# Batch 0's z and w2 transposed by DMA instead of by TensorE, in a Fourier filter with a maxout MoE

## The chip, the cores and the metric

The kernel runs on one core of a Trainium2 chip. A core has TensorE (PE; the profile shows its weight loads apart as PEld), VectorE (DVE), ScalarE (ACT), GpSimd (POOL) and SyncE (SP), which here only issues DMAs. The metric is device time in microseconds (us) of one execution; a median is taken over several. Profiled executions are told by their span, from the first to the last instruction.

## What is computed

```
X = np.fft.rfft(x, axis=1)                        # x: 8 batches, 3072 positions, 256 channels
Y = X * (filt_r + 1j * filt_i)[None, :, :]
x2 = np.fft.irfft(Y, n=3072, axis=1).reshape(24576, 256)
g = np.maximum(x2 @ w1, x2 @ w2)                  # hidden width 1024
out = g @ w_out                                   # 24576 x 256, float32
```

## The kernel before

The Fourier transform of 3072 points is split as 96 x 32 and done by matmuls with tables of sines, in bf16: a stage of 96 points, a stage of 32 points, the product with the filter, and the two stages back. For batches 1 to 7 the axes change places by DMAs through DRAM (`ad` and `zd`). Batch 0 has nothing to hide such a round trip behind, so it changes axes on TensorE: `s1t` and `t1` on the way in, `s3t` and `t2` on the way back.

`s3t(v, ...)` (L560, v = 0 to 5) is the third stage of batch 0. It leaves z with channels in the partitions; ACT and, for half of v = 4 and 5, DVE copy it from PSUM to the tile `zT` (128 partitions; two channel halves, 32 positions m, 96 values k). `t2(c, engines)` (L582, c = 0 to 7) turns the eight 128 x 96 squares of four positions on PE and copies them to `zr[0]` (96 partitions). `s4(tt)` (L454) does the last stage for tile tt of batch 0: eight matmuls of `zr[0]` with the table `G1`, copied by ACT and DVE to `y`. A batch has eight tiles of 384 positions, and tile tt needs just what `t2(tt)` wrote.

The MoE of a tile follows. Since max(a, b) = b + max(a - b, 0), `moe_h` (L476) computes relu(y (w1 - w2)) in eight blocks j, and `moe_o` (L501) adds this times w_out and y times M, where M = w2 w_out. `prep_m` (L308) makes M with 16 matmuls from `w2T`, the transposed w2: its first eight use the first half of the channels, its last eight the second. `prep_t(jp)` (L300) makes `w2T`: eight PE transposes and an ACT copy for each of two halves of the hidden axis. The input of these, `w2b`, is w2 cast to bf16 by POOL (`cast_w2`, L290), behind POOL's other set-up work. The result of `moe_o` is copied from PSUM to `ot`, and `out_block` (L491) writes it to DRAM: by POOL's queue, for the last two tiles by SP's.

The order of all this is written out by hand. Every engine runs its instructions in the order in which the program gives them. Set-up and batch 0's transform come first; then a loop runs over tiles and their eight blocks, and a step is 8 times the tile's number in its batch plus the block. At each step `moe_h` of this tile and `moe_o` of the tile before are issued, and what two tables, `mid` and `todo`, hold for the step. In batch 0 they hold, among others: `t2` of 1 at step 1, of 2 at step 7, of 3 at step 8, of 4 to 7 at steps 22, 32, 40 and 48; `prep_t` at steps 7 and 8; `prep_m` at step 9; `f1` (L323), the first stage of batch 1, whose results SP writes to `ad`, up to step 13; then `f1_read` (L340), which reads them back; the `visit`s of batch 1's middle stages from step 25; loads of batch 2's x into `XF` by SP (`load_xf`, L91) and their folding by POOL (`fold`, L101). `s4` of the next tile is issued at a tile's block 4. `s4g` is the last stage for batches 1 to 7; that of batch 1 reads what SP wrote to `zd` and read back.

Pools: the buffers of set-up (`init`, and `pq0` for the products) are given back by `setup.close()` (L686), and the pools opened behind it use their place. `zT` has one of two buffers of `bpool` before.

Of the kernel before, what the change touches and what calls it, by code (L numbers as in the profile page):

```python
# [8 lines left out]
FP32 = mybir.dt.float32  # L9
BF16 = mybir.dt.bfloat16  # L10
# [17 lines left out]
def kernel(  # L28
# [16 lines left out]

    const = ctx.enter_context(tc.tile_pool(name="const", bufs=1))
    C1 = const.tile([NP, 96], BF16)
    G1 = const.tile([96, NP], BF16)
    U = const.tile([128, NU, 64], BF16)
    VP = const.tile([128, NW, 2, 64], BF16)  # L50
    VQ = const.tile([128, NW, 2, 64], BF16)
# [18 lines left out]
    pso = ctx.enter_context(tc.tile_pool(name="pso", bufs=2, space=bass.MemoryType.PSUM))  # L70
    zrpool = ctx.enter_context(tc.tile_pool(name="zrpool", bufs=2))
    setup = ExitStack()
    init = setup.enter_context(tc.tile_pool(name="init", bufs=1))
    pq0 = setup.enter_context(tc.tile_pool(name="pq0", bufs=6))
    ctx.enter_context(tc.manual_schedule())

    xb = {}
# [76 lines left out]
    jb = init.tile([128, 16], FP32)  # L154
    cid = init.tile([128, 128], FP32)

    hv = init.tile([128, 2, 1], FP32)
    load_x(0, 0, 1)
    G.iota(pid, pattern=[[1, 1]], base=0, channel_multiplier=1, allow_small_or_imprecise_dtypes=True)
# [32 lines left out]

    def table_ct():
        G.memset(CT, 0.0)
# [54 lines left out]
        S.activation(U[:, NW * h:NW * h + NW], uv[:, NW * h:NW * h + NW], AF.Sin, bias=zero, scale=TWO_PI)  # L249

    def table_g():
        pg = ps.tile([96, NP], FP32, tag="ps", name="pg")
        TE.matmul(pg, C1, I128[0:NP, 0:NP], start=True, stop=True)
        S.activation(G1, pg, AF.Copy)

    def table_v(h, q):
# [40 lines left out]
        js = slice(256 * q, 256 * q + 256)  # L297
        engine.tensor_tensor(Wd[:, :, js], w1f[:, :, js], w2f[:, :, js], OP.subtract)

    def prep_t(jp):  # L300
        pt = ps.tile([128, 4, D], BF16, tag="ps", name="pt")
        for ji in range(4):
            for dc in range(2):
                j = 4 * jp + ji
                TE.transpose(pt[:, ji, 128 * dc:128 * dc + 128], w2b[:, dc, 128 * j:128 * j + 128], I128)
        S.activation(w2T[:, 4 * jp:4 * jp + 4], pt, AF.Copy)

    def prep_m():  # L308
        pm_ = ps.tile([128, 2, D], FP32, tag="ps", name="pm_")
# [144 lines left out]
    def s4(tt):  # L454
        b, i = divmod(tt, 8)
        y_ = ypool.tile([128, 2, 384], BF16, tag="yt", name="y_")
        for dc in range(2):
            py = ps.tile([128, 4, NP], FP32, tag="ps", name="py")
            for m in range(4):
                TE.matmul(py[:, m], zr[b][:, 4 * i + m, 128 * dc:128 * dc + 128], G1, start=True, stop=True)  # L460
# [30 lines left out]
    def out_block(tt, c):  # L491
        b, i = divmod(tt, 8)
        dst = out[b * N:(b + 1) * N].rearrange("(c p i m) d -> c i p (m d)", c=3, p=32, i=8)[c, i]
        E = G if tt < 8 * B - 2 else nc.sync
        E.dma_start(out=dst, in_=ot[tt // 2][:, 3 * (tt % 2) + c])  # L495


    FIRST = ([(c, e) for c in (0, 2) for e in range(8)] + [(c, e) for c in (0, 2) for e in (8, 9)]
             + [(1, e) for e in range(10)])

    def moe_o(tt, k0, k1):  # L501
        y_, g_ = yt[tt], gt[tt]
        for k in range(k0, k1):
            c, e = divmod(k, 10) if tt else FIRST[k]
            n = e if tt else (e + 2) % 10
            q = 3 * tt + c
            blk = slice(128 * c, 128 * c + 128)
            if e == 0 and (q % 2 == 0 or q == 24 * B - 1):
# [6 lines left out]
            if e == 9 and q >= 24 * B - 2:  # L515
                e = q % 6
                if q % 2 == 0:
                    S.activation(ot[tt // 2][:, e], p_, AF.Copy, scale=SCALE)
                else:
                    S.activation(ot[tt // 2][:, e, 0:112], p_[:, 0:112], AF.Copy, scale=SCALE)  # L520
                    V.tensor_scalar(ot[tt // 2][:, e, 112:D], p_[:, 112:D], SCALE, None, OP.mult)
# [37 lines left out]

    def s3t(v, pq):  # L560
        pool, tag = (ps, "ps") if v % 2 else (pso, "po")
        pz = [pool.tile([128, 2, 2, 2, 2, NM], FP32, tag=tag, name="pt%d" % g) for g in range(2)]
        for _ in range(2 if v == 1 else 1):
            TE.matmul(pz[0].rearrange("p i s r c m -> p (i s r c m)"), W1[:, 0:128], W1, start=True, stop=True)
        for i in range(2):
            for s in range(2):
                for dc in range(2):
                    for q, tab in enumerate((VP, VQ)):
                        for g in range(2):
                            TE.matmul(pz[g][:, i, s, :, dc], pq[s][64 * g:64 * g + 64, q, i, 128 * dc:128 * dc + 128],  # L570
                                      tab[64 * g:64 * g + 64, 2 * v + i, s].rearrange("p (r m) -> p r m", r=2),
                                      start=(q == 0), stop=(q == 1))
        zv = zT.rearrange("p c m (w g) q -> p w g (c m) q", g=2)
        for g in range(2):
            o_ = zv[:, 2 * v:2 * v + 2, g]
            i_ = pz[g].rearrange("p i s r c m -> p i (c m) (s r)")
            if v >= 4 and g == 1:
                V.tensor_copy(o_, i_)
            else:
                S.activation(o_, i_, AF.Copy)  # L580

    def t2(c, engines):  # L582
        if c == 0:
            zr[0] = zrpool.tile([96, NM, D], BF16, tag="zr", name="zr")
        n = 4 // len(engines)
        for k, engine in enumerate(engines):
            pr = ps.tile([96, n, D], BF16, tag="ps", name="pr")
            m0 = 4 * c + n * k
            for m in range(n):
                for dc in range(2):  # L590
                    TE.transpose(pr[:, m, 128 * dc:128 * dc + 128], zT[:, dc, m0 + m].rearrange("p u q -> p (u q)"),  # L591
                                 I128)
            if engine is V:
                V.tensor_copy(zr[0][:, m0:m0 + n], pr)
            else:
                S.activation(zr[0][:, m0:m0 + n], pr, AF.Copy)

    def spin(n):
        for _ in range(n):
# [96 lines left out]
    f1(1, 1, V)  # L696
    spin(1)
    s4(0)
# [46 lines left out]
    for b in range(1, B):  # L745
# [59 lines left out]
```

## Time and profile before

| what | value |
|---|---|
| time, median of 3 runs (lowest, highest) | 499.26 us (497.63, 505.28) |
| time of the profiled execution | 500.08 us |
| its span | 498.3 us |
| PE busy in the span | 482.5 us, 97% |
| DVE, ACT, POOL busy | 336.0, 320.0, 257.9 us |
| batch 0's t2: PE matmuls | 64, 0.219 us each, from 36.7 to 89.3 us |
| its DVE copies | 8, 0.42 to 0.69 us |
| prep_t: PE matmuls | 16, 0.219 us each, from 42.7 to 45.2 us |
| its ACT copies | 2, 1.024 us each |
| prep_m: PE matmuls | 16, 0.272 us each, from 46.4 us |

How to read it: busy time is what the profile attributes to instructions; matmuls overlap, so eight transposes in a row take 0.61 us, not eight times 0.219. Rows of the timeline give the start, the length to the end of the last instruction of a merged row, engine, line, operation, written and read tile, shape and count; what stands in brackets at the end is the idle time before, and what ended it. The rows of the table by stage give the stretch, its length, then busy time and count for PE, PEld, DVE, ACT and POOL, the clock that PE was granted, the mean busy share of the 16 DMA engines, and what they moved in GB/s.

### The profile page before, as it was taken

To read this page: it belongs to the slowest core of one execution; us is meant where nothing else is said; L and a number is where in the kernel's file an instruction comes from. 1 tells how busy PE (TensorE), PEld (TensorE's weight loads), DVE (VectorE), ACT (ScalarE), POOL (GpSimd) and SP (SyncE) were. 2 spreads that over 40 slices of the span, in tenths; PEclk is the share of its full clock that TensorE was granted. 3 is DMA by queue.
4 is the path that set the end of the run, shared out by engine and by line. 5 is a ranking of instruction groups with operands and counts; after the bars stand their busy time and mean duration, and the time that the engine had idled before them with its cause. 6 is when DMAs were issued, how large, how long until landed. Compare 5 with 4: busy or idle time off the path is not lost.

```text
span 498.3 us, 14113 instructions
## 1 busy us (share of the span) xinstructions
PE 482.5 (97%) x5749; PEld 352.4 (71%) x5749; DVE 336.0 (67%) x536; ACT 320.0 (64%) x666; POOL 257.9 (52%) x342
## 2 busy tenths in 40 slices
PE   7689999999999999999999999999999999999996
PEld 3447777767777777777777777776777777777775
DVE  7786788467865688458765688557873688555542
ACT  5777478666866667666866677666766656464542
POOL 8695559535846394537737196446842212222220
PEclk9989999999999999999999999999999999999999
DMA  8989699898789886897789977897776834531112
GB/s 124 166 232 213 201 231 297 246 240 223 243 268 216 201 255 186 252 224 179 236 255 230 201 211 216 269 204 192 225 231 177 180 102 128 160 117 66 64 63 86
DMA packets 76482, 97.30 MB, mean 195 GB/s; under 512 B 7841, under 2 KB 54210, under 8 KB 75042
## 3 DMA queue, kind: packets, MB, share of 16 engines
q1 hardware_dynamic: 63218, 66.80, 52.0%
q0 software_dynamic: 13200, 29.60, 21.6%
q8 instruction: 45, 0.74, 0.7%
q14 instruction: 19, 0.16, 0.1%
HBM read 53.87 MB, written 47.19 MB: 203 GB/s over the span
## 4 chain that ended last, share of the span: by engine, by line
PE 89%; DMA 4%; POOL 3%; issue 1%; DVE 1%; ACT 1%; SPq 0%; POOLq 0%; DVEq 0%
PE po L514 34%; PE ph L482 33%; PE po L512 8%; PE pz L408 5%; PE pc L443 3%; PE pa L355 2%; PE px L384 2%; DMA xb<-in_x_dram 2%; POOL pq L390 1%; DMA zd<-zt 1%; DMA zr<-zd 1%; DVE F L128 1%; PE pr L591 1%; POOL xb L89 1%; PE pa L330 1%
## 5 line engine op out<-in xcount | busy, mean ns | idle before, releaser
L514 PE MATMUL po<-Wo,gt 128*128 128x256 bf16 x1536 | 263.8, 273 | 0.0
L486 ACT ACTIVATE gt<-ph 128x384 bf16<-128x384 f32 x356 | 175.0, 496 | 138.2 <-PE ph L482 134.6
L514 PEld LDWEIGHTS <-gt 128*128 128x128 bf16 x1536 | 145.4, 98 | 66.9 <-issue 12.0
L495 POOL DMA_DIRECT2D out_dram<-ot x186 | 102.7, 557 | 159.4 <-DVE ot L530 136.6
L390 DVE TENSOR_TENSOR pq<-px,F 128x1024 bf16<-128x1024 f32 x91 | 106.9, 1219 | 25.7 <-PE px L384 25.4
L484 DVE TENSOR_SCALAR gt<-ph 128x384 bf16<-128x384 f32 x156 | 84.2, 552 | 52.3 <-PE ph L482 46.1
L482 PEld LDWEIGHTS <-Wd 128*128 128x128 bf16 x1024 | 99.4, 98 | 15.1 <-issue 1.2
L104 POOL TENSOR_TENSOR xb<-XF 128x512 bf16<-128x512 f32 x48 | 61.2, 1276 | 63.1 <-DMA XF<-in_x_dram 57.0
L530 DVE TENSOR_SCALAR ot<-po 128x512 f32<-128x512 f32 x83 | 57.1, 687 | 35.0 <-PE po L514 35.0
L105 POOL TENSOR_TENSOR xb<-XF 128x512 bf16<-128x512 f32 x48 | 61.0, 1271 | 0.0
L359 ACT ACTIVATE at<-pa 128x512 bf16<-128x512 f32 x96 | 51.8, 613 | 3.4 <-PE pa L355 3.3
L412 ACT ACTIVATE zt<-pz 128x512 bf16<-128x512 f32 x84 | 45.6, 595 | 5.7 <-PE pz L408 1.9
L448 ACT ACTIVATE ce<-pc 128x384 f32<-128x384 f32 x56 | 23.7, 491 | 7.8 <-PE pc L443 7.1
L408 PE MATMUL pz<-pq,VP 64*64 64x256 bf16 x336 | 22.2, 281 | 0.0
L408 PE MATMUL pz<-pq,VQ 64*64 64x256 bf16 x336 | 21.2, 269 | 0.0
L384 PE MATMUL px<-bt,U 64*64 64x256 bf16 x384 | 19.8, 275 | 1.2 <-ACT VQ L279 0.7
L408 PEld LDWEIGHTS <-VP 64*64 64x64 bf16 x336 | 10.1, 105 | 13.3 <-issue 12.7
L355 PE MATMUL pa<-xb,CT 64*64 64x512 bf16 x192 | 18.0, 377 | 0.0
L443 PEld LDWEIGHTS <-zr 48*128 48x128 bf16 x896 | 12.9, 93 | 5.1 <-issue 4.4
L443 PE MATMUL pc<-G,zr 48*128 48x48 bf16 x896 | 15.2, 180 | 0.6 <-DMA zr<-zd 0.6
L384 PEld LDWEIGHTS <-U 64*64 64x64 bf16 x384 | 10.5, 107 | 3.9 <-issue 3.6
L601 PE MATMUL pd<-W 128*128 128x512 bf16 x28 | 9.1, 436 | 1.5 <-DVE zero L150 1.5
(379 smaller groups left out, 628.4 us busy)
## 6 DMA issues: line engine op xcount, KB each, us to landing
out_dram<-ot POOLq DMA_DIRECT2D x186, 128.0 KB, 3.8
XF<-in_x_dram SPq DMA_DIRECT2D x96, 192.0 KB
ad<-at SPq DMA_DIRECT2D x56, 192.0 KB
zd<-zt SPq DMA_DIRECT2D x42, 256.0 KB
zr<-zd SPq DMA_DIRECT2D x56, 192.0 KB
bt<-ad SPq DMA_DIRECT2D x13, 768.0 KB
WS<-in_moe_w_dram SPq DMA_DIRECT2D x4, 512.0 KB
xb<-in_x_dram POOLq DMA_DIRECT2D x8, 192.0 KB, 6.6
```

The source lines that it names most:

```text
L104: G.tensor_tensor(t_[:, 0], f[:, 0], f[:, 1], OP.add)
L105: G.tensor_tensor(t_[:, 1], f[:, 0], f[:, 1], OP.subtract)
L359: S.activation(at[:, m0:m0 + 2], pa[g], AF.Copy)
L390: E.tensor_tensor(pq, px.rearrange("p (o i) d -> p o i d", o=1).to_broadcast([128, 2, 2, D]), F[:, :, 2 * v:2 * v + 2, s], OP.mult)
L408: TE.matmul(pz[g][64 * s:64 * s + 64, i], tab[64 * g:64 * g + 64, 2 * v + i, s], pq[s][64 * g:64 * g + 64, q, i], start=(q == 0), stop=(q ...
L412: S.activation(zt[:, :, g], pz[g], AF.Copy)
L482: TE.matmul(ph, Wd[:, dc, 128 * j:128 * j + 128], y_[:, dc], start=(dc == 0), stop=(dc == 1))
L484: V.tensor_scalar(gt[tt][:, j], ph, 0.0, None, OP.max)
L486: S.activation(gt[tt][:, j], ph, AF.Relu)
L495: E.dma_start(out=dst, in_=ot[tt // 2][:, 3 * (tt % 2) + c])
L514: TE.matmul(p_, g_[:, n - 2, blk], Wo[:, n - 2], start=(e == 0), stop=(e == 9))
L530: V.tensor_scalar(ot[tt // 2][:, e - 1:e + 1], po[q // 2 % 2], SCALE, None, OP.mult)
```

## The change

- z of batch 0: `zT` is laid out as eight tiles of [2 channel halves, 4 positions, 128 values], the 96 values padded with zeros to two halves of 64. The table `G1` gets the same 128 rows (a padded sine table `CP`, two more sines). `t2` is now only for tile 0 (its four positions), still by PE, in two pieces copied by DVE and ACT. Tiles 1 to 7 are transposed by two DMAs of SP from `zT` to `zr[0]`: one for tile 1 (eight squares of 128 x 128) and one for tiles 2 to 7 (48 squares).
- The last zT copy (v = 5) is made in two pieces, tile 0's first.
- w2: `prep_t` is now two DMA transposes of SP, one for each half of the channels (eight squares each), given at step 5. `prep_m` stays at step 9.
- Buffers: `zT` has a pool of its own in the set-up's place, `pq0` has four buffers instead of six and is used from v = 4 on, and the pools behind `setup.close()` are opened in another order, so that `ot` lies where `zT` was.
- The end: the last block of the last tile is computed in two halves of 128 columns in tiles of PSUM of their own, copied by ACT and by DVE and written by a DMA from ACT and one from SP; another of the last tile's blocks is written from ACT's queue.

On SP's queue the two transposes of z stand ahead of the first `ad` writes; two `ad` writes follow, then the two of w2, then the rest as before.

```diff
-    G1 = const.tile([96, NP], BF16)
+    G1 = const.tile([128, NP], BF16)
...
+    zT = setup.enter_context(tc.tile_pool(name="zt0", bufs=1)).tile([128, 8, 2, 4, 128], BF16, name="zT")
     init = setup.enter_context(tc.tile_pool(name="init", bufs=1))
-    pq0 = setup.enter_context(tc.tile_pool(name="pq0", bufs=6))
+    pq0 = setup.enter_context(tc.tile_pool(name="pq0", bufs=4))
...
+        V.memset(CP, 0.0)
+        for s in range(2):
+            S.activation(CP[:, 64 * s:64 * s + 48].rearrange("p (g w r) -> p g w r", g=2, r=2),
+                         uc.rearrange("p (w g s) r -> p s g w r", g=2, s=2)[:, s], AF.Sin, bias=zero[0:NP],
+                         scale=TWO_PI)
...
-        TE.matmul(pg, C1, I128[0:NP, 0:NP], start=True, stop=True)
+        TE.matmul(pg, CP, I128[0:NP, 0:NP], start=True, stop=True)
...
-    def prep_t(jp):
-        pt = ps.tile([128, 4, D], BF16, tag="ps", name="pt")
-        for ji in range(4):
-            for dc in range(2):
-                j = 4 * jp + ji
-                TE.transpose(pt[:, ji, 128 * dc:128 * dc + 128], w2b[:, dc, 128 * j:128 * j + 128], I128)
-        S.activation(w2T[:, 4 * jp:4 * jp + 4], pt, AF.Copy)
+    def prep_t():
+        for dc in range(2):
+            nc.sync.dma_start(out=w2T[:, :, 128 * dc:128 * dc + 128], in_=w2b[:, dc], transpose=True)
...
-        E = G if tt < 8 * B - 2 else nc.sync
+        E = G if tt < 8 * B - 2 else S if (tt, c) == (8 * B - 1, 0) else nc.sync
...
+    def last_block(tt):
...
+        for h in range(2):
+            cols = slice(128 * h, 128 * h + 128)
+            pl = ps.tile([128, 128], FP32, tag="ps", name="pl")
...
+            if h == 0:
+                S.activation(ot[tt // 2][:, 5, cols], pl, AF.Copy, scale=SCALE)
+                S.dma_start(out=dst[:, :, cols], in_=ot[tt // 2][:, 5, cols])
+            else:
+                V.tensor_scalar(ot[tt // 2][:, 5, cols], pl, SCALE, None, OP.mult)
+                nc.sync.dma_start(out=dst[:, :, cols], in_=ot[tt // 2][:, 5, cols])
...
+        for o0, o1 in ((0, 1), (1, 8)) if v == 5 else ((0, 8),):
+            for g in range(2):
...
-    def t2(c, engines):
-        if c == 0:
-            zr[0] = zrpool.tile([96, NM, D], BF16, tag="zr", name="zr")
...
+    def t2(engines):
+        zr[0] = zrpool.tile([128, 8, 2, 4, 128], BF16, tag="zr", name="zr")
...
+    def t2_dma(o0, o1):
+        nc.sync.dma_start(out=zr[0][:, o0:o1].rearrange("p o c m d -> p (o c m) d"),
+                          in_=zT[:, o0:o1].rearrange("p o c m k -> p (o c m k)"), transpose=True)
...
-    zT = bpool.tile([128, 2, NM, NU, 4], BF16, tag="bt", name="zT")
+    V.memset(zT.rearrange("p o c m (s k) -> p (o c m s) k", s=2)[:, :, 48:64], 0.0)
...
-        pool = pq0 if v > 2 else pqpool
+        pool = pq0 if v > 3 else pqpool
...
     setup.close()
+    opool = ctx.enter_context(tc.tile_pool(name="opool", bufs=2))
+    zpool = ctx.enter_context(tc.tile_pool(name="zpool", bufs=3))
     apool = ctx.enter_context(tc.tile_pool(name="apool", bufs=3))
-    zpool = ctx.enter_context(tc.tile_pool(name="zpool", bufs=3))
-    opool = ctx.enter_context(tc.tile_pool(name="opool", bufs=2))
...
-    t2(0, (V, S))
+    t2((V, S))
+    t2_dma(1, 2)
+    t2_dma(2, 8)
...
-    plan(0, 1, t2, 1, (V,))
-    plan(0, 7, prep_t, 0)
+    plan(0, 5, prep_t)
     plan(0, 9, prep_m)
-    for c, n in ((2, 7), (4, 22), (5, 32), (6, 40), (7, 48)):
-        plan(0, n, t2, c, (V,))
...
-    mid[0, 8] = [(t2, (3, (V,))), (prep_t, (1,))]
```

More of the change, by code (lines that the diff above doesn't have):

```diff
@@ L155 @@
     cid = init.tile([128, 128], FP32)
+    CP = init.tile([NP, 128], BF16)
     hv = init.tile([128, 2, 1], FP32)
@@ L251, in table_g @@
     def table_g():
-        pg = ps.tile([96, NP], FP32, tag="ps", name="pg")
-        TE.matmul(pg, C1, I128[0:NP, 0:NP], start=True, stop=True)
+        pg = ps.tile([128, NP], FP32, tag="ps", name="pg")
+        TE.matmul(pg, CP, I128[0:NP, 0:NP], start=True, stop=True)
         S.activation(G1, pg, AF.Copy)
@@ L459, in s4 @@
             for m in range(4):
-                TE.matmul(py[:, m], zr[b][:, 4 * i + m, 128 * dc:128 * dc + 128], G1, start=True, stop=True)
+                TE.matmul(py[:, m], zr[b][:, i, dc, m], G1, start=True, stop=True)
             o_ = y_[:, dc].rearrange("p (t m) -> p t m", m=4)
@@ L493, in out_block @@
         dst = out[b * N:(b + 1) * N].rearrange("(c p i m) d -> c i p (m d)", c=3, p=32, i=8)[c, i]
-        E = G if tt < 8 * B - 2 else nc.sync
+        E = G if tt < 8 * B - 2 else S if (tt, c) == (8 * B - 1, 0) else nc.sync
         E.dma_start(out=dst, in_=ot[tt // 2][:, 3 * (tt % 2) + c])
+    def last_block(tt):
+        y_, g_ = yt[tt], gt[tt]
+        b, i = divmod(tt, 8)
+        dst = out[b * N:(b + 1) * N].rearrange("(c p i m) d -> c i p m d", c=3, p=32, i=8)[2, i]
+        for h in range(2):
+            cols = slice(128 * h, 128 * h + 128)
+            pl = ps.tile([128, 128], FP32, tag="ps", name="pl")
+            for n in range(10):
+                if n < 2:
+                    TE.matmul(pl, y_[:, n, 256:384], M[:, n, cols], start=(n == 0), stop=False)
+                else:
+                    TE.matmul(pl, g_[:, n - 2, 256:384], Wo[:, n - 2, cols], start=False, stop=(n == 9))
+            if h == 0:
+                S.activation(ot[tt // 2][:, 5, cols], pl, AF.Copy, scale=SCALE)
+                S.dma_start(out=dst[:, :, cols], in_=ot[tt // 2][:, 5, cols])
+            else:
+                V.tensor_scalar(ot[tt // 2][:, 5, cols], pl, SCALE, None, OP.mult)
+                nc.sync.dma_start(out=dst[:, :, cols], in_=ot[tt // 2][:, 5, cols])
     FIRST = ([(c, e) for c in (0, 2) for e in range(8)] + [(c, e) for c in (0, 2) for e in (8, 9)]
@@ L507, in moe_o @@
             blk = slice(128 * c, 128 * c + 128)
-            if e == 0 and (q % 2 == 0 or q == 24 * B - 1):
+            if q == 24 * B - 1:
+                if e == 0:
+                    last_block(tt)
+                continue
+            if e == 0 and q % 2 == 0:
                 po[q // 2 % 2] = pso.tile([128, 2, D], FP32, tag="po", name="po")
@@ L514, in moe_o @@
                 TE.matmul(p_, g_[:, n - 2, blk], Wo[:, n - 2], start=(e == 0), stop=(e == 9))
[L515 to L521, printed above, removed]
+            if e == 9 and q == 24 * B - 2:
+                S.activation(ot[tt // 2][:, q % 6], p_, AF.Copy, scale=SCALE)
                 out_block(tt, c)
@@ L561, in s3t @@
         pool, tag = (ps, "ps") if v % 2 else (pso, "po")
-        pz = [pool.tile([128, 2, 2, 2, 2, NM], FP32, tag=tag, name="pt%d" % g) for g in range(2)]
+        pz = [pool.tile([128, 2, 2, 2, 8, 2, 4], FP32, tag=tag, name="pt%d" % g) for g in range(2)]
         for _ in range(2 if v == 1 else 1):
-            TE.matmul(pz[0].rearrange("p i s r c m -> p (i s r c m)"), W1[:, 0:128], W1, start=True, stop=True)
+            TE.matmul(pz[0].rearrange("p s i r o c m -> p (s i r o c m)"), W1[:, 0:128], W1, start=True, stop=True)
         for i in range(2):
@@ L572, in s3t @@
                                       start=(q == 0), stop=(q == 1))
[L573 to L578, printed above, removed]
-            else:
-                S.activation(o_, i_, AF.Copy)
-    def t2(c, engines):
-        if c == 0:
-            zr[0] = zrpool.tile([96, NM, D], BF16, tag="zr", name="zr")
[L585 to L596, printed above, removed]
+        for o0, o1 in ((0, 1), (1, 8)) if v == 5 else ((0, 8),):
+            for g in range(2):
+                c0 = 24 * g + 4 * v
+                o_ = zT[:, o0:o1].rearrange("p o c m (s k) -> p s (o c m) k", s=2)[:, :, :, c0:c0 + 4]
+                i_ = pz[g][:, :, :, :, o0:o1].rearrange("p s i r o c m -> p s (o c m) (i r)")
+                if v >= 4 and g == 1:
+                    V.tensor_copy(o_, i_)
+                else:
+                    S.activation(o_, i_, AF.Copy)
@@ new lines, in t2 @@
+    def t2(engines):
+        zr[0] = zrpool.tile([128, 8, 2, 4, 128], BF16, tag="zr", name="zr")
+        for k, engine in enumerate(engines):
+            pr = ps.tile([128, 2, 2, 128], BF16, tag="ps", name="pr")
+            for m in range(2):
+                for dc in range(2):
+                    TE.transpose(pr[:, dc, m], zT[:, 0, dc, 2 * k + m], I128)
+            o_ = zr[0][:, 0, :, 2 * k:2 * k + 2]
+            if engine is V:
+                V.tensor_copy(o_, pr)
+            else:
+                S.activation(o_, pr, AF.Copy)
```

4 lines of the change are left out of this document (2 added, 2 removed).

## The prediction

> **What bounds the kernel now.** I read four views in this order: the page's chain that ended last, the timeline from 36 to 48 us, the table by stage, and SP's queue with the rows of its DMAs' landing.
>
> ```profile
> PE 89%; DMA 4%; POOL 3%; issue 1%; DVE 1%; ACT 1%; SPq 0%; POOLq 0%; DVEq 0%
> ```
>
> The chain lies on PE for 89% of the span, so an instruction taken from PE shortens the run, unless something off PE ends last at that place. The place in question is the start of batch 0's MoE:
>
> ```profile
> 41.16 2.03 POOL L291 CAST w2b<-WS 128x1024 bf16<-128x1024 f32 x2
> ...
> 42.70 0.61 PE L305 MATMUL pt<-I,w2b 128*128 128x128 bf16 x8
> ...
> 43.14 0.61 PE L591 MATMUL pr<-I,zT 128*96 128x128 bf16 x8
> ...
> 44.80 0.61 PE L305 MATMUL pt<-I,w2b 128*128 128x128 bf16 x8
> ...
> 45.44 1.02 ACT L306 ACTIVATE w2T<-pt 128x1024 bf16<-128x1024 bf16 x1 [0.22 <-PE pt L305]
> ...
> 46.44 1.91 PE L312 MATMUL pm__1151<-Wo,w2T 128*128 128x256 bf16 x16
> ```
>
> See the order: POOL ends the cast of w2 at 43.2, PE transposes, ACT copies until 46.46, and prep_m starts on PE at 46.44, all but released by that copy. From the cast's end to prep_m it is 3.2 us. PE is in order, so whatever holds prep_m holds all MoE work behind it. In the table by stage I read clock, DMA share and GB/s (the last three columns):
>
> ```profile
> 22.00:24.00 2.00, 0.41 (x7) 0.14 (x6) 2.00 (x2) 1.85 (x5) 0.00 (x0) 1.00 0.80 203
> 24.00:26.00 2.00, 1.19 (x49) 0.70 (x53) 1.76 (x4) 1.45 (x4) 1.80 (x1) 0.66 0.05 12
> 26.00:28.00 2.00, 2.00 (x70) 1.10 (x71) 2.00 (x3) 1.24 (x3) 1.99 (x3) 0.50 0.70 160
> 28.00:30.00 2.00, 1.92 (x67) 1.22 (x62) 2.00 (x3) 1.62 (x4) 2.00 (x2) 0.98 1.00 371
> 38.00:40.00 2.00, 2.00 (x21) 1.34 (x22) 1.72 (x4) 1.47 (x3) 2.00 (x2) 1.00 1.13 155
> 40.00:43.00 3.00, 3.00 (x31) 1.94 (x29) 2.91 (x7) 2.06 (x5) 3.00 (x5) 1.00 1.18 206
> 48.00:50.00 2.00, 2.00 (x17) 1.44 (x15) 0.41 (x1) 1.61 (x4) 0.00 (x0) 1.00 0.95 311
> ```
>
> Two things: the DMA engines are already full (share 0.95 to 1.18) just where the new transposes would run, and after PE had little to do from 22 on, its granted clock was 0.66 and 0.50 for some 4 us. Last, how long a DMA from SP takes to land:
>
> ```profile
> 52.67 1.79 SPq L338 DMA_DIRECT2D ad<-at  x3
> 56.84 3.04 SPq L344 DMA_DIRECT2D bt<-ad  x3
> ```
>
> ```profile
> 91.03 4.90 DMA zd<-zt
> ```
>
> The last of three ad writes (192 KB) is issued by 54.46 and the read that waits for it starts at 56.84, 2.4 us later; a zd write of 256 KB took 4.9 us.
>
> **The change, part by part.** The sum is made against the profiled execution: 500.08 us, of which 498.3 are span and 1.8 lie around it. It stands 0.8 above the median of the runs shown (499.26).
>
> *Up to the first tile.* DVE gets a memset of zT's padding (1024 words a partition; the 512-element memset of W took 0.48, so 0.96) from 16.1 to 17.1. It delays the first bt copy from 16.78 by 0.3; the copies have gaps of 0.20 twice, and the F copies behind them are released at 19.30 by a DMA. At most 0.1, taken as 0. The memset of CP and two sines sit in idle time of DVE (0.40 at 4.28) and ACT (1.77 at 6.06): 0. With two fewer buffers the products of v=3 now reuse those of v=1, read by PE until 28.35; DVE writes them at 29.08, POOL from 28.95: 0. The last zT copy is split, so PE's first transposes need only a piece of 64 elements a half instead of the 0.69 copy: PE is free at 36.15 rather than waiting to 36.65, but ACT's zr copy still follows an at copy: some 0.2 gained.
>
> *PE up to prep_m.* Gone are t2 of tiles 1 to 3 and both prep_t: five groups of eight transposes, 0.45 each on the chain (0.056 pitch): 2.25. DVE loses three copies of 0.68 and ACT two of 1.02. PE would stand at prep_m at 46.44 - 2.25 - 0.2 = 44.0. But w2T is not there then; it now comes by SP's queue, and that decides this place.
>
> *SP's queue.* In order: z's transposes (1,2) and (2,8) at about 36.75, when the second pieces of zT are written; two ad writes; the two w2 transposes, which wait for the cast (43.2); the next ad writes, x loads of batch 2, the bt reads. These last are held by a slow SP too, but the f1 products that feed them stand behind prep_m on PE, so they move along. prep_m's second half, 8 x 0.109 after its start, ran from 47.31 and needs the second w2 transpose. Calling its landing L, all behind prep_m shifts by L - 47.3.
> No row shows a transposing DMA; I bound L by bytes. Ahead of L on SP's queue: 56 squares of 32 KB (1.84 MB), ad 0.39 MB, w2 0.52 MB: 2.75 MB. The engines moved 2.89 MB from 36 to 50 in the run before (rate times time of its rows); less what SP then had, 1.58 MB is POOL's (x of batch 1, w_out). Together 4.33 MB. At the best rate seen, 371 GB/s, that ends 11.7 us after 36.75; at 311, 13.9; at 206, 21. I take 311, the rate nearest in time with SP's own loads on it, and add a landing of 1.8 (the ad's 2.4 less 0.6 of transfer): L = 52.5, a shift of +5.2. Bounds: 47.0 (nothing in the way: 43.2, landing 2.4, 0.9 for the second, rounded up) and 73.9 (SP's queue gets half of 155 GB/s: 35.3 us, and 1.8).
> [...]
>
> *The other waits.* s4(1) needs (1,2), 256 KB: landing 2.4 to 4.9 after 36.75, so 39.2 to 41.7, against PE's arrival at 40.92 - 0.45 - 0.2 = 40.3: a stall of 0 to 1.4, which only uses up part of the wait at prep_m. s4(2) needs (2,8), which lands ahead of w2. The first output copy of DVE (54.97) waits for (2,8) as well, since its tile lies where zT was: covered.
>
> *Clock.* A PE wait from 44 to 51 is longer than the lull before 24 to 28, where 4 us at half clock cost about 2 us of PE work. 0 if the lull is too short, 2 if it repeats; I take +1.0.
>
> *After prep_m.* Tiles 4 to 7: four groups of 0.45. The last, at 88.92, lies between PE's pz at 86.14 and the s4g at 101, where PE waited 0.56 for zr<-zd already; so it only lengthens that wait. Gain 1.35.
>
> *The end.* The last block's ten matmuls ended at 494.29, then ACT 0.26 and DVE 0.31 came one after the other, and SP issued at 494.9. In two halves with own banks, the last DVE copy can end near 494.65, and half as much is left to write, in 512-byte rows. Gain 0 to 0.6, taken 0.3. The (63,0) block's issue moves to ACT, which idles 2.02 before 493.23.
>
> **Sum:** +5.2 + 1.0 - 1.35 - 0.3 = +4.55, so 500.08 + 4.55 = 504.6. (PE's 2.45 ahead of prep_m is in L - 47.3: it turns into waiting.)
>
> **The rivals.** (A) *Faster: the transposes are hidden.* z's squares are through by the cast's end, and each w2 transpose lands as an ordinary DMA does: 43.2 + 3.6 (between 2.4 and 4.9) + 0.9 = 47.7. The shift is +0.4, no clock loss, and 500.08 + 0.4 - 1.65 = 498.8. It decides at L = 48.95: below, the change is faster. For it: a rate of 371 GB/s was seen, and SBUF to SBUF takes nothing from HBM. Against: the share of 1.13 to 1.18 at 155 to 206 GB/s in that stage.
> (B) The forecast, 504.6: L between 49.5 and 57.
> (C) *SP's queue becomes the bound.* Transposes run square by square, at about half of the 206 GB/s that the queues shared: 2.75 MB at 100 GB/s is 27.5 us, L = 66, a shift of +18.7, clock +2: 500.08 + 18.7 + 2 - 1.65 = 519.1. For it: a square is 128 rows of 256 bytes, and the page counts only 7,841 of 76,482 packets under 512 B; against: nothing in the trace shows a DMA from SP that slow. [...]
> (D) *It cancels:* L near 49, nothing to see, 500.1.
>
> **How the numbers follow.** A 0.30, B 0.43, C 0.20, D 0.07. The likeliest is B, 504.6; B's own range is 500.6 to 510. For 8 in 10 the range takes in A down to 497 (landing 2.4, t2 of tile 7 paying too, end 0.6) and the fast part of C up to 515. Some 2% is what a measurement of this kernel can tell from no change: against 499.26 that is 489.3 and 509.2. PE's whole saving is 4.05 + 0.5, so faster by over 2% has 0.01; C and B's upper end (L above 57) make slower by over 2% 0.23; the rest, 0.76, is within.
>
> **What would show it.** In the changed kernel's timeline: the start of prep_m's second half (47.31 before): at 47 to 48 A is right, 50 to 57 B, above 60 C. PE's idle time before the first w2T weight load should name a DMA w2T<-w2b; the clock in the 4 us behind it shows whether +1.0 was due. s4(1)'s wait on zr<-zT tells how long 8 squares take: 2.4 to 4.9 us from 36.75. SP's issue times of the 48-square transpose tell C at once if they are many us. From prep_m to 86 the distance of like instructions should shrink by 1.35. I am wrong if POOL's cast moves, if the squares (2,8) hold only their own queue and w2 passes freely, or if the end of zr<-zd at 101 moves by itself.

## The result, and the profile after

The changed kernel takes 529.32 us (median of 4 runs, 522.80 to 538.98) against 499.13 us before (4 runs): ratio 1.0553, interval 1.051 to 1.0596, slower. The ratio leaves out runs in a slower state, such as the one at 538.98, so it is below the quotient of the two medians (1.0605). Its profiled execution took 530.26 us, with a span of 528.5 us; the span of before was 498.3, so 30.2 us are to be found.

The page, in the lines that answer to those of before: the packets, SP's queue, the chain, and the group of prep_m (busy us and mean ns, then the idle time ahead of it).

```profile
DMA packets 85970, 99.65 MB, mean 189 GB/s; under 512 B 17201, under 2 KB 63698, under 8 KB 84530
...
q1 hardware_dynamic: 72418, 68.96, 54.7%
...
PE 79%; SPq 7%; DMA 7%; ACT 2%; POOL 2%; issue 1%; DVE 0%; POOLq 0%; ACTq 0%
...
L315 PE MATMUL pm__1116<-Wo,w2T 128*128 128x256 bf16 x16 | 3.6, 419 | 20.4 <-DMA w2T<-w2b 20.4
```

PE's share of the chain fell from 89 to 79%; SP's queue took 7% and DMAs 3% more. The packets under 512 B rose from 7,841 to 17,201: 72 squares of 128 rows of 256 bytes are 9,216 of them. (q1 is SP's queue.) One wait, of prep_m for the transposed w2, holds 20.4 of the 30.2 us. The timeline, first of SP's queue, then of PE's two stalls:

```profile
35.39 31.16 SPq L618 DMA_TRANSPOSE zr<-zT  x2
66.65 0.98 SPq L341 DMA_DIRECT2D ad<-at  x2
67.72 2.92 SPq L309 DMA_TRANSPOSE w2T<-w2b  x2
...
44.77 0.82 PE L463 MATMUL py<-G,zr 128*128 128x96 bf16 x8 [5.73 <-DMA zr<-zT]
...
71.47 3.60 PE L315 MATMUL pm__1116<-Wo,w2T 128*128 128x256 bf16 x16 [20.41 <-DMA w2T<-w2b]
```

The chain says the same in two pieces (start, us, what):

```profile
37.11 29.43 SPq L618
...
67.72 3.70 DMA w2T<-w2b
```

SP spent 29.4 us on issuing one DMA, that of the 48 squares: 1.57 MB, 53 GB/s. The w2 transposes stood behind it on the same queue. The table by stage (last three columns: PE's clock, DMA share, GB/s) shows what the 16 DMA engines did meanwhile:

```profile
36.00:38.00 2.00, 1.86 (x16) 1.01 (x15) 1.71 (x4) 1.49 (x4) 1.97 (x2) 1.00 1.02 164
...
46.00:48.00 2.00, 2.00 (x7) 0.97 (x6) 0.85 (x3) 1.02 (x2) 0.00 (x0) 0.50 1.18 28
...
54.00:58.00 4.00, 0.00 (x0) 0.00 (x0) 0.00 (x0) 0.00 (x0) 0.00 (x0) 0.50 1.14 64
58.00:62.00 4.00, 0.00 (x0) 0.00 (x0) 0.00 (x0) 0.00 (x0) 0.00 (x0) 0.50 1.01 76
62.00:64.00 2.00, 0.00 (x0) 0.00 (x0) 0.00 (x0) 0.00 (x0) 0.00 (x0) 0.50 1.35 69
64.00:66.00 2.00, 0.00 (x0) 0.00 (x0) 0.00 (x0) 0.00 (x0) 0.00 (x0) 0.50 1.12 242
66.00:68.00 2.00, 0.00 (x0) 0.00 (x0) 0.00 (x0) 0.00 (x0) 0.00 (x0) 0.50 1.30 297
```

A share over 1 at 28 GB/s: on average every engine has a packet in hand, and hardly a byte moves. At 64 us something ends, and the same queue runs at 242 to 297 GB/s. The counts of packets that began in each 2 us name it (256 B are the transposes; POOL's 4,096 B are batch 1's x; "before" has no transposes, and the output that POOL's queue writes there from 56 us on, in packets of the same size, is not counted):

```
us     after: 256 B / x, 4,096 B         before: x, 4,096 B
44-46           264 / 9                          84
46-48            94 / 8                          67
52-54            85 / 22                          0
58-60           213 / 24                          0
62-64           221 / 20                          0
64-66          1894 / 0                           0
66-68          2104 / 0                           0
```

In this stretch the loads that POOL's queue had through by 50 us before take until 64 us, and the transposes crawl as long as the loads last. Of the 1,655 transposing packets that began from 44 to 64 us, 1,021 took 40 ns at most, but 491 took 300 ns or more, and these make up 82% of the time of all; the mean is 158 ns, against 18 ns from 64 to 68 us. The 4,096 B packets suffer too: their median is 322 ns, as good as the 324 before, but their mean rose to 726 ns, from 348 before (44 to 50 us). Each holds the other up.

Where the 30.2 us arise along the run is read best by the delay, against before, of the first `moe_h` weight load of each tile:

```
tile           0      1      2      3      4      5      6      7      8      9 ...   40     41 ...   63
start before  38     44     55     61     70     79     88     95    103    110      330    338      485
delay      -1.72  +4.77 +27.75 +27.30 +27.29 +28.86 +28.84 +28.39 +30.78 +31.46   +31.49 +30.57   +30.66
```

The -1.72 at tile 0 is not a gain of the change: the version with the end part alone, whose set-up is that of before, stands at -1.66 there, and one with the changed set-up at +1.30. From there on, 6.5 us come at s4(1), 23.0 at prep_m, 1.6 at tile 4's end, 3.1 from tile 7 to 9; two groups of transposes give back 0.45 each (tiles 2 and 6). The waits of PE between 80 and 145 us tell of what the late ones are, first before, then after:

```profile
PE pc L443 <- DMA zr<-zd: 0.6, 1, 0.6
```

```profile
PE pc L446 <- DMA zr<-zd: 2.5, 2, 1.5
PE ph L485 <- ACT zt L415: 1.2, 2, 0.8
PE pa L358 <- POOL xb L106: 0.7, 1, 0.7
```

### The profile page after: what moved, and what is told of

Read it like the earlier page. It is cut to its first block, busy times and chain, and to the rows that moved or that the text cites. A ratio compares the mean times of both kernels' runs of the same rounds, so it can differ in the third digit from the quotient of the medians.

```text
span 528.5 us, 14001 instructions
## 1 busy us (share of the span) xinstructions
PE 486.8 (92%) x5687; PEld 352.3 (67%) x5687; DVE 333.0 (63%) x532; ACT 319.2 (60%) x667; POOL 258.6 (49%) x342
## 2 busy tenths in 40 slices
DMA packets 85970, 99.65 MB, mean 189 GB/s; under 512 B 17201, under 2 KB 63698, under 8 KB 84530
## 3 DMA queue, kind: packets, MB, share of 16 engines
HBM read 53.87 MB, written 47.19 MB: 191 GB/s over the span
## 4 chain that ended last, share of the span: by engine, by line
PE 79%; SPq 7%; DMA 7%; ACT 2%; POOL 2%; issue 1%; DVE 0%; POOLq 0%; ACTq 0%
PE po L540 30%; PE ph L485 28%; PE po L538 7%; SPq L618 6%; PE pz L411 4%; PE pc L446 3%; DMA zd<-zt 2%; PE px L387 2%; PE pa L358 2%; DMA XF<-in_x_dram 2%; DMA xb<-in_x_dram 2%; PE pt L591 1%; SPq L95 1%; DMA zr<-zd 1%; DMA w2T<-w2b 1%
## 5 line engine op out<-in xcount | busy, mean ns | idle before, releaser
L485 PEld LDWEIGHTS <-Wd 128*128 128x128 bf16 x1024 | 100.5, 99 | 16.7 <-issue 3.2
L336 DVE CAST at<-pa 96x512 bf16<-96x512 f32 x8 | 5.5, 684 | 27.8 <-PE pa L333 27.6
L315 PE MATMUL pm__1116<-Wo,w2T 128*128 128x256 bf16 x16 | 3.6, 419 | 20.4 <-DMA w2T<-w2b 20.4
L446 PE MATMUL pc<-G,zr 48*128 48x48 bf16 x896 | 15.5, 181 | 2.5 <-DMA zr<-zd 2.5
```

Source lines behind the costliest of these rows:

```text
L485: TE.matmul(ph, Wd[:, dc, 128 * j:128 * j + 128], y_[:, dc], start=(dc == 0), stop=(dc == 1))
```

## The experiments

Theory 1: transposing packets and another queue's packets hold each other up in the DMA engines, and that is the whole slowness. Theory 2: a DMA of 48 squares is slow by its size. Theory 3: z's layout makes it slow. All shifts below are those of tile starts, as in the table above.

**Batch 1's x loads early.** All four `load_x(1, c, 2)` moved ahead of the loop `for v in (1, 0, 2)`, away from the transposes.

```diff
+    for c in (0, 2, 4, 6):
+        load_x(1, c, 2)
     for v in (1, 0, 2):
         pqs[v] = products(v)
-        if v == 0:
-            load_x(1, 0, 2)
...
-    load_x(1, 2, 2)
```

> The changed kernel with one move: POOL issues its four loads of batch 1's x ahead of its products, not between set-up work, so that they are through when z's transposes start. Theory 1 (transposes and POOL's loads hold each other up in the DMA engines; alone, 56 squares go at the 240 to 300 GB/s seen at 64 to 68 us): only w_out's load is still in the way, the 48-square DMA lands at 45 to 48 us instead of 66, w2T at 48 to 51 instead of 71, the time is 499 to 506 us. Theory 2 (a DMA of 48 squares is slow by its size) and theory 3 (z's squares are slow by their layout): landing at 66 as before, 526 to 532 us.

508.37 us (506.11 to 511.88), ratio 1.0166 (1.0078 to 1.0254). The same two DMAs of z, unchanged:

```profile
35.53 12.21 SPq L618 DMA_TRANSPOSE zr<-zT  x2
48.94 2.94 SPq L309 DMA_TRANSPOSE w2T<-w2b  x2
```

12.2 us instead of 31.2, and its packets run at 2,178 and 2,267 per 2 us from 44 us on, once w_out's 512 B packets are through. Size and layout are the same, so theories 2 and 3 fall as the main cause. The rate of the transposes alone, in the table by stage:

```profile
44.00:48.00 4.00, 3.56 (x17) 2.16 (x18) 1.55 (x3) 1.51 (x3) 1.90 (x5) 0.50 1.28 284
```

The time is still above the 499 to 506 of theory 1: about 21 of the 30 us are gone, and 8.4 stay against the 499.98 us measured beside it.

**w_out early too**, against the first experiment:

```diff
-    for c in (0, 2, 4, 6):
+    for c in (0, 2):
+        load_x(1, c, 2)
+    load_wo()
+    for c in (4, 6):
         load_x(1, c, 2)
...
-    load_wo()
```

> As the kernel with the early x loads, with the load of w_out moved up as well, between them. Theory 1: nothing is left in the engines beside z's transposes, 1.8 MB at 240 to 300 GB/s: landing at 43 to 46 us, w2T at 47 to 49, time 497 to 503 us. Theories 2 and 3: 526 to 532 us.

509.55 us, ratio 1.0183 (1.0113 to 1.0253); z's issue 11.61 us. Nothing is won, and the stretch was not cleared as the expectation had it: the last x packets now come behind w_out (72, 66 and 11 per 2 us from 38 to 44 us), beside SP's own loads of w1 and w2. The transposes crawl again in it (195 and 430 per 2 us from 40 to 44 us), and behind it run at 1,896 to 2,265. Also w1 and w2 land later and POOL's subtractions wait for them (6.9 us).

**The control: x loads early in the kernel before.** The diff of the first experiment, in a kernel with no transposing DMA.

> The kernel before with batch 1's four x loads issued ahead of the products, as in the first experiment, and no transposing DMA at all: the control for it. Theory 1 (transposing packets and POOL's loads hold each other up, and nothing else in that experiment cost time): 498 to 501 us, so that the 1.0166 there is the transposes' own, the 12.2 us issue of the six tiles and the wait at prep_m for w2T. Rival (the early loads themselves cost, because w1 and w2 land later and GpSimd's subtractions wait for them, 3.8 us there): 503 to 508 us, ratio 1.008 or more.

501.58 us, ratio 1.0043 (1.0008 to 1.0079): in between. PE's longest wait shows why, POOL's late `Wd`:

```profile
PE ph L482 <- POOL Wd L298: 3.0, 2, 1.9
```

So the early loads cost some 2 us by themselves. At tile 9 the run with transposes is at +8.19 and the control at +3.79: 4.4 us are left to transposes that only w_out's packets disturb, 1.8 us of it in the wait at prep_m and 2.65 between tiles 7 and 9, where zr is late. So theory 1 holds for most of the slowness, not for the whole.

**The 48 squares as six DMAs** of eight, at the same place:

```diff
-    t2_dma(2, 8)
+    for o in range(2, 8):
+        t2_dma(o, o + 1)
```

> The changed kernel with the 48-square DMA given as six of eight squares. Theory 1: the same packets meet the same loads, tile 7's squares still land at about 66 us, the time is 525 to 533 us. Theory 2: each of the six takes 1.3 to 1.7 us as w2's did, the last lands by 47, w2T by 50, the time is 500 to 506 us. Theory 3: as theory 1.

512.54 us in a single run, between what the two theories gave.

```profile
37.78 15.47 SPq L618 DMA_TRANSPOSE zr<-zT  x7
54.44 2.71 SPq L309 DMA_TRANSPOSE w2T<-w2b  x2
```

The packets alternate: 1,032 and 1,016 transposing ones from 40 to 44 us, then none for 2 us while 82 of POOL's pass, then transposes again. With short DMAs the two queues took turns here and mixed little; the long one is mixed with the loads from 44 us to their end. So length mattered here beside another queue: 15.5 us of issue for the seven short DMAs, 31.2 for the two with the long one.

**w2 alone by DMA**, in the kernel before, with z by PE.

```diff
-    plan(0, 7, prep_t, 0)
+    plan(0, 5, prep_t)
...
-    mid[0, 8] = [(t2, (3, (V,))), (prep_t, (1,))]
+    mid[0, 8] = [(t2, (3, (V,)))]
```

> The kernel before with w2 alone transposed by SP's two DMAs (given at step 5), z by PE. Theory 1: the 16 squares start at 43 us amid POOL's x loads, which ran until 48; both are held up, w2T lands at 52 to 60 us, the time is 502 to 512 us. Theories 2 and 3: eight squares at a time are quick, w2T lands at 46 to 48 us, the time is 498 to 501 us.

508.61 us, ratio 1.0147 (1.0083 to 1.021): the time that theory 1 gave. prep_m started at 50.06, though, between the landings that the theories gave (52 to 60, and 46 to 48). Two DMAs of 0.26 MB, which take 2.9 us when POOL's queue is silent, take twice that beside its last x loads, and prep_m waits 4.9 us:

```profile
42.83 5.83 SPq L302 DMA_TRANSPOSE w2T<-w2b  x2
```

**z alone by DMA**: the changed kernel, with w2 by PE in its old place.

```diff
-    plan(0, 5, prep_t)
+    plan(0, 7, prep_t, 0)
...
+    mid[0, 8] = [(prep_t, (1,))]
```

> The changed kernel, but w2 transposed by TensorE in its old place: z by SP's DMAs alone. Theory 1: the six-tile DMA still takes about 30 us to issue, beside POOL's loads; s4(1) still waits some 5.7 us, prep_m no longer waits for w2T, and s4(2), at 51.7 us before and so near 57 here, waits for the landing near 68: 11 us. 499.1 + 5.7 + 11 + 0 to 3 = 515 to 520 us, ratio 1.032 to 1.041. Rival (the whole loss came from w2's queueing behind z; the z tiles would be in time by themselves): 503 to 507 us, the 5.7 us of s4(1) alone.

527.55 us, higher than theory 1 had it; its times scatter (516.4 to 536.1), so no ratio is given. The profiled run is one of the longer (530.49), so the size of its waits is rough. It has 35.06 us of issue for z, and a stall that the expectation did not have:

```profile
PE pa L337 <- DMA xb<-in_x_dram: 13.8, 1, 13.8
PE py L467 <- DMA zr<-zT: 5.0, 2, 4.8
```

It was f1 that waited, for x, until 68.45. So PE came to s4(2) only at 73.8, and waited another 0.2 for z there: the wait that was expected lies hidden in that for x, and loads and transposes were late together. w2's place in the queue is not what the loss hangs on: without it even the shortest of the four runs loses 17 us.

**Which queue, which packets?** Three single runs start from the version with early x loads and put three plain copies of 0.79 MB from DRAM to DRAM, whose data nobody uses, beside z's transposes (added work): on ACT's queue in 8,192 B packets, the same in 512 B packets, and on POOL's queue.

```diff
+    def dummy(E, b, c, n):
+        src = x[b].rearrange("(p m) d -> p m d", m=NM)
+        E.dma_start(out=dd[:, 4 * c:4 * c + 4 * n], in_=src[:, 4 * c:4 * c + 4 * n, :])
...
+    for c in (2, 4, 6):
+        dummy(S, 2, c, 2)
     t2_dma(2, 8)
```

> The first experiment (batch 1's x loads early) and, on ACT's DMA queue just ahead of the six-tile DMA, three plain copies of 0.79 MB each from DRAM to DRAM whose data nobody uses (added work). If packets of any second queue hold transposing packets up, the six tiles' issue grows from 12.2 us to 22 us or more and the time to 515 us or more. If only POOL's queue does so, it stays at 12 to 15 us and the time at 507 to 512 us.

> The run with plain copies on ACT's queue, with the same bytes in packets of 512 B instead of 8,192 B (each of the three copies cut in two halves of the rows; added work). If a transposing packet has to wait for whatever packet of the other queue is being moved, shorter packets must free it sooner: the six tiles' issue falls from 26.1 us to 14 to 19 us, and the time from 525 us to 509 to 516 us. If it is the other queue's bytes or its mere presence that counts: 24 us or more again, and 522 us or more.

> As the run with ACT's queue, with the same three plain copies on POOL's queue, just after the products' share of POOL (added work; they convert nothing). If it is POOL's queue that holds transposing packets up, or any second queue: six tiles' issue of 20 us or more, and the time 515 us or more. If it is the converting of fp32 to bf16 in POOL's loads: 12 to 16 us, and the time 507 to 513 us.

524.95, 518.62 and 513.92 us. SP's rows for ACT's queue with long packets, then with short ones:

```profile
37.36 26.14 SPq L618 DMA_TRANSPOSE zr<-zT  x2
```

```profile
37.70 19.57 SPq L618 DMA_TRANSPOSE zr<-zT  x2
```

Their rows from 50 to 54 us, in the same order:

```profile
50.00:54.00 4.00, 0.00 (x0) 0.00 (x0) 0.00 (x0) 0.00 (x0) 0.00 (x0) 0.50 0.91 170
```

```profile
50.00:54.00 4.00, 2.61 (x9) 1.22 (x9) 1.05 (x2) 1.46 (x3) 0.00 (x0) 0.50 1.21 301
```

```
packets begun per 2 us:  256 B / ACT's 8,192 B         256 B / ACT's 512 B
50-52                        144 / 31                      893 / 634
52-54                         75 / 45                      863 / 838
60-62                       2213 / 0  (copies over)
```

ACT's queue does it as well as POOL's (26.1 us of issue instead of 12.2), and with no conversion of types: neither POOL's queue nor the conversion is the cause. (A few of w_out's packets, 19 to 11 per 2 us, still lay on POOL's queue until 50 us.) With 512 B packets the crawl is gone: transposes run at 440 per us, and the sum of both is 301 GB/s instead of 170. As both runs copy the same bytes, what the transposes suffer from is the long packets of the other queue. (The 491 slow packets of the changed kernel have their like here: of 1,142 transposing packets from 44 to 60 us beside 8,192 B ones, 321 took 300 ns or more, and beside 512 B ones, from 48 to 56 us, none of 3,465.) The issue of 19.6 us is a little above what was expected (14 to 19), and so is the time.

The run with POOL's queue did not answer its question: the packets of the copies began only near 49 us, when z was through. They met w2's transposes instead, whose issue took 7.76 us in place of 2.9. No transposing packet began from 50 to 56 us, while the queues together moved 403 GB/s.

**The end part alone**: `last_block`, its copies and its writes, put into the kernel before.

> The kernel before with the end part alone: the last block in two halves on a bank of their own, its copies on ACT and VectorE, its writes on ACT's and SP's queues. The prediction's term was -0.3 us (0 to -0.6); from the last matmul's end to the span's end the two traces so far have 4.0 us before and 3.5 us after, so -0.5. Expected 498.5 to 499.3 us, ratio 0.998 to 1.000. Rival: the halves cost TensorE more than the shorter tail gives back, 499.5 to 500.5 us.

498.79 us, ratio 0.9984 (0.9967 to 1.0000), -0.8 us: at the lower edge of what was expected, and the only part of the change that was not a loss when measured alone.

**Making use of it.** Six versions leave the early tiles of z to TensorE and give SP only late ones, one DMA a tile.

*Tiles 4 to 7 after steps 9 to 12*, w2 by TensorE, with the end part:

```diff
-    t2((V, S))
-    t2_dma(1, 2)
-    t2_dma(2, 8)
+    t2(0, (V, S))
...
+    plan(0, 12, t2_dma, 4, 5)
+    plan(0, 11, t2_dma, 5, 6)
+    plan(0, 10, t2_dma, 6, 7)
+    plan(0, 9, t2_dma, 7, 8)
```

> A version made from what the runs have shown: the changed kernel's layout and end part, w2 by TensorE as before, z's tiles 0 to 3 by TensorE, and tiles 4 to 7 by four single-tile DMAs, one each after the steps 9 to 12 (46 to 52 us), when POOL's loads are nearly done. Four groups of eight transposes leave TensorE (4 x 0.45 = 1.8 us), the end gives 0.5. Theory 1: each of the four issues in 1 to 3 us, nothing waits for them, 496.5 to 498.5 us, ratio 0.995 to 0.999. Rival: SP's queue, held by them, delays batch 1's ad and the XF loads behind them, and waits at 100 to 140 us take the gain back or more: 499 to 503 us.

502.82 us, ratio 1.0063 (1.0040 to 1.0087). That is in the rival's range, but for another reason: VectorE's first copy into `ot`, which lies over zT's memory, waited for the last transpose, and PE behind it.

```profile
PE po L542 <- DVE ot L553: 4.8, 1, 4.8
```

The tile starts show the rest: +6.68 at tile 4, then 6.23, 5.71, 5.26, and 4.52 at tile 8: 2.2 us gained by three groups off TensorE and, in the last step, the fourth and the 0.6 us wait for zr that the kernel before has there.

*The same with w2 by DMA*:

```diff
+    plan(0, 5, prep_t)
...
-    plan(0, 9, prep_m)
+    plan(0, 11, prep_m)
```

> As the version with four late tiles, and w2 transposed by SP's two DMAs after step 5 with prep_m two steps later (after step 11 instead of 9). Theory 1: w2T lands near 50.5 us as in the run with w2 alone, prep_m would stand near 46.9 us (the 2.25 us of w2's transposes gone), so it waits about 2 us after step 11 at most and the 2.25 us come out even or better: 495 to 499 us. Rival: the crawl of w2T beside POOL's last loads also delays x and f1, and the time is 501 to 506 us.

508.19 us, ratio 1.0184 (1.0152 to 1.0216), above both ranges that were given. The `ot` wait again (5.9 us), 1.7 us of PE for w2T. Here too the delay falls from 8.66 at tile 4 to 6.50 at tile 8.

*The `ot` wait taken away*: other buffers, one of XF's among them, over zT's memory.

```diff
+    late = ctx.enter_context(tc.tile_pool(name="late", bufs=1))
     opool = ctx.enter_context(tc.tile_pool(name="opool", bufs=2))
...
+        if XF[(8 * b + c) % 3] is None:
+            XF[0] = late.tile([128, 1408], FP32, name='XF0')[:, 0:1024].rearrange('p (a b d) -> p a b d', a=2, b=2)
```

> The version with four late tiles, with one wait taken away that had nothing to do with transposing: the first ot buffer lay over zT's memory, and VectorE's copy into it waited 5.8 us for the last zr<-zT (PE 4.8 us behind it). Here zpool's, cepool's and a late XF buffer's memory lie over zT instead, and ot beside it. If the prediction's gain after prep_m (0.45 us per group of eight transposes taken off TensorE) is real: 502.8 - 4.8 = 498.0 us, with the end part 497 to 498.5, ratio 0.995 to 0.999. If SP's queue, held by the transposes, takes it back elsewhere: 499.5 us or more, ratio 1.000 or more.

506.85 us, ratio 1.0124 (1.0083 to 1.0164): slower, not faster. The next wait was right behind:

```profile
PE px L393 <- DMA bt<-ad: 4.6, 1, 4.6
PE pc L452 <- DMA zr<-zd: 2.4, 3, 1.6
```

The four DMAs stand among f1's `ad` writes on SP's queue, and the `bt` reads issue at 62.98 instead of 56.84 us. In the first version the `ot` stall had hidden that. By the tile starts this version is still ahead of it at tile 7 (+4.00 against +5.26) and behind at tile 9 (+6.95 against +4.52), after the waits for zr.

*Five tiles*: `plan(0, 8, t2_dma, 3, 4)` in place of tile 3's `t2`.

> As the version with four free tiles, with tile 3 by a single-tile DMA too, after step 8, ahead of the others. If each group taken off TensorE is worth its 0.45 us: 0.4 us less than the four-tile version, 496.5 to 498 us. If step 8 is too early, beside POOL's last x loads: the first DMA issues over 3 us, the XF loads behind it come later, and the time is that of the four-tile version or up to 3 us more.

508.11 us, ratio 1.0157 (1.0125 to 1.0189), the second of the two cases given; the wait for `bt` is 6.4 us.

*Four tiles behind the `bt` reads*: the four `plan(0, 14, t2_dma, c, c + 1)` stand behind `plan_f1`, whose read is of step 14.

> As the version with four free tiles, with the four single-tile DMAs not amid f1's ad writes but behind the three bt reads of step 14 (about 60 to 66 us, after POOL's x loads and ahead of the XF loads of step 15). If all that cost time there was SP's queue holding batch 1's ad and bt (PE waited 4.6 us for bt, 6.4 us with five tiles), the wait goes and what is left is the prediction's gain: 1.8 us for four groups off TensorE and 0.5 for the end: 496.5 to 498.5 us, ratio 0.994 to 0.999. If the XF loads, now some 5 us later, pass the delay on to batch 1's zd and zr (waits at 100 to 140 us): 499.5 to 503 us, ratio 1.000 or more.

506.72 us, ratio 1.0116 (1.0067 to 1.0164). The wait for `bt` is gone, but s4(4), which stands at 62 us before, waits for its tile instead:

```profile
PE py L469 <- DMA zr<-zT: 5.5, 1, 5.5
PE pc L452 <- DMA zr<-zd: 2.5, 2, 1.3
```

*Three of them*: tile 4 by `plan(0, 14, t2, 4, (V,))` again.

> As the version with the DMAs behind the bt reads, with tile 4 by TensorE again (after step 14): s4(4) stands at 62 us, ahead of those DMAs, and PE waited 5.5 us for it there; s4(5) stands at 75.6 us and the three remaining DMAs land near 67. If the gain behind prep_m is real and that wait was the whole loss: 3 x 0.45 = 1.35 us and 0.5 for the end, 497 to 498.5 us, ratio 0.995 to 0.999. If the XF loads, some 4 us later behind the three DMAs, pass it on to zd and zr of batch 1 (PE waited 2.5 us for zr there, 0.6 us before): 499.5 to 502 us.

507.46 us, ratio 1.0148 (1.0110 to 1.0187), above both ranges. Now no reader of z waits. But SP's queue has the XF loads of step 15 10 us later (70.39 instead of 59.92: 8.7 us for the three DMAs, 2.1 for zT's memory, where that buffer now lies), and what comes of XF is late all the way, +7.94 at tile 10:

```profile
PE pz L417 <- ACT zt L421: 2.3, 1, 2.3
PE pc L452 <- DMA zr<-zd: 2.1, 2, 1.2
...
PE pa L364 <- POOL xb L108: 0.9, 1, 0.9
```

No version with SP transposing in this stretch beat the kernel before.

## Why the prediction was wrong

It gave 504.6 us (497 to 515) and 76% to "within 2%"; 529.3 was measured. The side and the place were right, the size was not. By its own steps:

- **"I take 311, the rate nearest in time with SP's own loads on it": the step that failed.** L was put at 52.5; the first w2 transpose landed at 71.42 (67.72 + 3.70 in the chain) and prep_m's second half began some 1.8 later, near 73.2, close to the upper bound (73.9) that the text had worked out and left out of its range. The DMA engines were priced as one pipe that shares its bytes, and the row that gave 311 (48 to 50 us) has 288 packets of SP's queue and only 8 of POOL's x: it shows hardly any mixing. The runs show 28 to 76 GB/s for both queues together while transposes are mixed with POOL's x loads, 151 to 181 with ACT's 8,192 B copies, 279 to 290 GB/s for transposes alone (2,178 and 2,267 packets per 2 us), and 301 when the other queue has short packets. The pipe's rate depended on what it was shared with.
- **Rival C** had the right queue and the right sign, with a reason that only half fits: squares are not slow by themselves (279 to 290 GB/s alone, in the run with early x loads). At its 100 GB/s it gave 519.1; the trace has 53 for the 48 squares. It had a chance of 0.20.
- **s4(1): a stall of 0 to 1.4, "covered".** It was 5.73: tile 1's 256 KB, issued from 35.4 us on, landed at 44.7, 9 us later, behind w_out's packets (431 and 384 per 2 us from 38 to 42 us), and then among packets of the 48 squares: 1,510 transposing packets had begun by 44 us, more than tile 1's 1,024. That it would only use up a part of the wait at prep_m was right: prep_m starts with the landing, whenever PE comes.
- **Clock +1.0.** prep_m alone took 3.60 us instead of 1.91 at a clock of 0.50, +1.7. The versions give the price by itself: with the free tiles, PE idle for 4.6, 6.4 and 5.5 us (four, five, behind `bt`) delayed the next tile by 6.67, 8.65 and 7.39, so 1.9 to 2.3 us on top, the term's upper end.
- **After prep_m -1.35.** The term is real: 0.45 a group at the tile starts, and 2.2 us from tile 4 to 8 in the two versions where nothing else was late. In the changed kernel 0.9 of it shows, and 4.6 us of later waits for zt, xb and zd eat it (1.6 and 3.1 in the table of tile starts); these are waits for what comes by SP's queue, which was late by then. The text had that wait at 101 us only as the place where the last group's gain is lost; with the queue late it costs more than it hides.
- **The end -0.3**: right as far as it can be told. From the last tile's start to the span's end the changed kernel gains 0.5; the part alone gained 0.8 in the times (0 to 1.6), of which its trace shows 0.1 in that place.
- **The range** left out C's upper half, though the upper bound of its one unknown price (73.9) came to 527 by its own sum: 500.08 + 26.6 + 2 - 1.65. An unmeasured kind of DMA put on a queue that carries everything else deserved that end. Two slips in the working change little: POOL's queue moved 1.66 MB from 36 to 50 us, not 1.58, and 2.75 MB at half of 155 GB/s is 35.5 us, not 35.3.

Not settled: why mixing costs so much. Of the 491 slow packets, 322 took between 300 and 360 ns, about as long as one long packet (322). That would fit a transposing packet that has to wait for a long one, but no run here shows what it waits for, nor why the long ones grow slower too.

## What to carry to other kernels

Before moving work from an engine to a DMA, look which other queues have packets in flight in that stretch and how long these are: here a transposing DMA beside another queue's long packets ran at a fraction of its speed (28 to 76 GB/s for both queues beside POOL's loads, 279 to 290 alone) and slowed POOL's loads as well (726 ns a packet on average instead of 348), and beside 512 B packets it suffered far less (301 GB/s for both). Then read what stands behind it on the same queue, since the issue of a long DMA held the queue here for as long as its packets crawled (29.4 us); in the one run that tried it, several short DMAs mixed less than one long one (15.5 us of issue instead of 31.2). And take a wait away only after looking at the next one behind it: three versions in a row freed one wait here and found others behind it that cost as much or more.

## What the runs showed of the hardware

- Issuing a long transposing DMA held SP while most of its packets went: when the issue of the 48 squares ended at 66.54 us, 5,669 of z's 7,168 packets had begun. It took 10.8 us with the x loads out of the way, 29.4 us beside them. Eight squares took 1.2 to 1.6 us to issue where nothing disturbed them; tile 1's eight took 1.7 us though they landed only 9 us after the start.
- A DMA share of 1.0 to 1.6 went with 28 to 76 GB/s (46 to 64 us): share is time with a packet in hand, not bytes.
- The transposes took nothing from HBM: it read 53.87 MB and wrote 47.19 MB before and after, while the DMAs moved 97.30 MB before and 99.65 MB after.
- Transposing packets of 256 B: 18 ns alone, about 1,130 per us over the 16 engines, 290 GB/s; the row of 44 to 48 us in the run with early x loads has 284 GB/s at a share of 1.28.
- After PE had been idle for 4.8 us, its clock was 0.50 for 4 us of work (62 to 66 us in the version with four late tiles).
